# Windowed attention and a multiplicative feed-forward net in one kernel: attention of batches 2 and 3 regrouped by token halves, and more transposes by DMA

## The chip, the core and the metric

The kernel runs on one core of one Trainium2 chip. Its metric is the device time of one execution in microseconds (us). The engines of the core have these names: PE is the matrix engine (TensorE; PEld is its weight load), ACT is ScalarE, DVE is VectorE, POOL is GpSimd, SP is SyncE. POOL issues the loads, SP the DMA transposes and the stores of the output. All times are the slowest core's, and here there is one core.

## What is computed

Four batches of eight heads, 768 tokens and head size 64 go through attention in which a token sees the first four tokens (the sinks) and the 128 tokens that end with itself. The result, as 3072 rows of 512, goes through two gates, their product, and two matrices:

```python
scores = scale * np.matmul(q, k.transpose(0, 1, 3, 2))
keep = is_sink | in_window            # n_sink = 4, window = 128
scores = np.where(keep, scores, -1000000000.0)
a = softmax(scores); attn = np.matmul(a, v)
x = attn.transpose(0, 2, 1, 3).reshape(3072, 512)
h = (x @ w1) * (x @ w2) @ w3          # 512 -> 1024 -> 1024
out = h @ w_out                       # 1024 -> 512
```

## The kernel before

**Tiles.** Tokens come in blocks of 128 (six to a batch), three blocks make a chunk c of 384 tokens, and two heads make a pair r (four pairs). P is 128, NP 4, NC 2, QC 3. Scores are made with k blocks on the partitions and q along the free axis, for a pair of heads at once.

**Stages.** First w3 and w_out are folded into one matrix w3o (L333 to L389: transposes L339 and L370, matmuls L347 and L377), so that the last two products become one. For each batch then: q and k are transposed into qkT (on PE for batches 0 and 1, L427 and L450, copied out of PSUM; by DMA transposes on SP for batches 2 and 3, L468). The four sink keys of all heads stand in a small tile ksbd; its scores with q (L504) and their exponentials es (L509) belong to all heads together. A *visit* makes the scores of one or two *strips* (L547); a strip is a set of up to four blocks of 128 x 128 for two heads, and has one exponential on ACT (L560) and one masking product on DVE (L566). Attention times v (L618) gathers a chunk and a head pair in PSUM, with a column that sums the weights; DVE inverts the sum (L628) and normalizes into xs (L633). The six transposes per two head pairs that turn xs into xT are made on PE (L654, copied by L658) or, for batch 3, by three DMA transposes per chunk (L674). Each chunk then has eight pairs of gate matmuls of 384 columns (L698), a copy (L705), a product (L713), and three output blocks (L728) that are copied (L737) and stored (L745).

**Which strips.** `pieces` (L393) lists (k block, q block, number of q blocks, place in the strip) per head pair. Kind 0 (batches 0 and 1) has four strips a pair, two for each token half. Kind 1 (batches 2 and 3) has three strips a pair of 3, 4 and 4 blocks, twelve a batch, taken two at a time in six visits; the first visit needs k and q of the whole batch. The sink scores of kind 1 are one group of 512 columns ahead of the visits; those of kind 0 are two groups of 128 and 384 columns.

**Memory.** q and k of batches 2 and 3 lie in the tile `big`, over w3 and w_out, which are dead once the fold is done (L391). PSUM holds two score tiles sc, one av and three general tiles mm. Rings of tiles: three ex, six am, three xs, three xT, three o_sb.

**What sets the order.** The program is ordered when it is built. Each piece of work is an `Op` (L125) with an engine, a cost in us, dependencies and a priority; a list planner (L749 to L847) lets time pass, and on each engine emits the op that can begin first, at equal readiness the one of lower priority number (`when`, L415, spreads the attention of batch b over the projection of batch b - 1). The engines then run their instructions in this order, each in its own queue, with semaphores for the true data dependencies, which the framework puts in from the tiles that an instruction reads and writes. `Op.deps` is read by the planner. PE gaps that the planner foresees before 45 us are filled with matmuls on zeros (L807). `load` (L155) gives a load's cost, `dma["at"]` the planner's time of the DMA queue; at most eight POOL loads are in flight (L796, and lane semaphores on the chip). `unsure` (L760) adds 1.5 to 3.5 us to a load that ends after 40 us. A DMA transpose takes 1.3 us of the planner's DMA time (`TUS`, `turn`).

**The load list.** `LOADS` (L238) is the order of POOL's work by hand: `k2-4` is k of batch 2, token block 4; `v0-2` likewise; `q0-0-4` is the first half of batch 0, heads 4 to 7 (heads 0 to 3 come by SP and ACT, L210); `w3j-2-4` two column blocks of the first rows of w3, `w3-5` a row block of w3, `wo-6-8` two row blocks of w_out, `w0` to `w3` quarters of w1 and w2. `ident`, `tri` and `pick` are small constants that POOL computes. A load of q, k or v of one block moves 256 KB of float32 and writes 128 KB of bfloat16.

Of the kernel before, what the change touches and what calls it, by code (L numbers as in the profile page):

```python
# [21 lines left out]
def kernel(  # L22
# [22 lines left out]
    P = 128  # L45
# [23 lines left out]
    maskt = home("maskt", [P, 1, 7 * P])  # L69
# [55 lines left out]
    class Op:  # L125
        def __init__(self, eng, us, fn, deps=(), prio=0.0, takes=(), frees=(), lat=0.0,
                     margin=0.0, src=0.0):
            self.us_on = {eng: us} if isinstance(eng, str) else dict(zip(eng, us))
            self.eng, self.fn, self.prio = eng, fn, prio
            self.deps, self.takes, self.frees = list(deps), list(takes), list(frees)  # L130
            self.lat, self.margin, self.src = lat, margin, src
            self.done = self.slot = self.after = None
            self.serial = len(ops)
            ops.append(self)
# [18 lines left out]
    dma = dict(at=3.45, fetch=False)  # L153
# [12 lines left out]
    KA, LEAD, SPREAD = 3, -120, 0.6  # L166
    FOLD_J, FOLD_I = 990, 980
    C_MAJOR = 2
    QK_BY_DMA = (2, 3)
    X_BY_DMA = ((3, 0), (3, 1))  # L170
# [62 lines left out]
    for r in range(2):  # L233
# [4 lines left out]
    LOADS = """w3j-1-2 tri k0-0-4 q0-0-4 wo-0-1 wo-2-4 ident v0-2 w3j-2-4 w3j-6-8 w3j-0-1 wo-1-2 pick  # L238
        v0-1 wo-4-6 w3j-4-6 v0-0 w3-7 wo-6-8 w3-6 w3-5 w3-4 q0-1-0 k0-1-0 w0 w3-3 v0-5 w2 v0-3 w1
        k1-1 k1-0 w3 k1-3 q1-1 v0-4 k1-2 q1-0 q2-0 q1-2 k1-4 v1-0 q1-4 v1-5 k2-0 v1-2 v1-4 k2-3  # L240
        v1-1 q1-5 k2-2 q2-2 v1-3 q2-4 q2-1 q1-3 k2-1 k1-5 v2-5 v2-2 k2-5 v2-0 k2-4 v3-1 q2-5 q2-3
        q3-0 k3-3 v2-4 k3-2 v2-1 v2-3 k3-0 k3-4 k3-5 q3-2 k3-1 v3-2 q3-5 q3-1 v3-4 q3-3 q3-4 v3-3
        v3-0 v3-5"""

    def masks(part):
        m = maskt[:, 0, :].rearrange("p (k q) -> p k q", q=P)
        if part:
            for k in (1, 3, 4, 6):
                nc.vector.tensor_copy(m[:, k, :], tri[:])
            nc.vector.memset(m[0:4, 4:6, :], 1.0)  # L250
        else:
            for k in (0, 2, 5):
                nc.vector.tensor_scalar(m[:, k, :], tri[:], -1.0, 1.0, op0=ALU.mult, op1=ALU.add)

# [49 lines left out]
    op_mask = Op(DVE, 0.6, lambda: masks(1), [op_mask], prio=3)  # L304
    op_cols = Op(DVE, 0.35, pick_cols, [op_pick], prio=3)
# [100 lines left out]
    for b in range(B):  # L406
        kind = 0 if b < C_MAJOR else 1
# [33 lines left out]
        elif b not in QK_BY_DMA:  # L441
            for c in range(NC):
                for r in range(NP):
                    x = []

                    def tps(b=b, c=c, r=r, x=x):
                        tp = transposed(x[0].slot["mm"], 6 * P).rearrange("p (s j m) -> p s j m", s=2, m=P)
                        for s, src in ((0, kN[b]), (1, qN[b])):
                            for j in range(QC):
                                nc.tensor.transpose(tp[:, s, j, :],  # L450
                                                    src[:, QC * c + j, r * P:(r + 1) * P], ident[:])

                    def tpc(T=T, c=c, r=r, x=x):
                        copy(
                            T[:, r, :, c * TOK:(c + 1) * TOK],
                            transposed(x[0].slot["mm"], 6 * P).rearrange("p (s m) -> p s m", s=2))
                    a = Op(PE, cols(P, 6), tps,
                           [got[n, b, QC * c + j] for n in "kq" for j in range(QC)] + [op_ident] + war,
                           when((r / 4 + c) / 2 - 0.1 if kind == 0 else r / 4 + c / 50 - 0.1, 0), takes=["mm"])
                    x.append(a)  # L460
                    tp_of[c, r] = Op(EITHER, (act_us(6 * P), dve_us(6 * P, 2)), tpc, [a], base + 1, frees=[(a, "mm")])
        if b not in QK_BY_DMA:
            tdep = lambda c, r: [tp_of[c, r]] + ([tp_of[0, r]] if c else [])
        else:
            for kb in range(NB):
                for s, n, src in ((0, "k", kN), (1, "q", qN)):
# [3 lines left out]
                    tp_of[s, kb].turn = TUS  # L470
            if b + 1 in QK_BY_DMA:
                seen = []
                for o in in_big:
                    if o.batch == b:
                        seen.append(next(t for t in tp_of.values() if o in t.deps))
                    elif o.batch == b + 1:
                        o.deps += seen[:-3]
            tdep = lambda c, r: [tp_of[s, kb] for s in range(2) for kb in range(3 * c + 3)]
# [17 lines left out]
        groups = [(2, 3), (3, 6)] if kind == 0 else [(2, 6)]  # L496
        op_es = {}
        for q0, q1 in groups:
# [12 lines left out]
            cs = {(qb // QC) for qb in range(q0, q1)}  # L511
            a = Op(PE, cols(w) + 0.22, ss, [op_sk] + sum([tdep(c, r) for c in cs for r in range(NP)], []) + warv,
# [6 lines left out]
        tasks = []  # L519
        if kind == 0:  # L520
            for c in range(NC):
                for r in range(NP):
                    two = [(r, 2 * c), (r, 2 * c + 1)]
                    tasks += [two] if c or b else [[t] for t in two]
        else:
            flat = [(r, t) for r in range(NP) for t in range(3)]
            tasks = [flat[i:i + 2] for i in range(0, 12, 2)]
        block, sc_ops = {}, []
        am_left = {}
        for n_v, visit in enumerate(tasks):  # L530
            x = []
            us = 0.13
            deps = []
            for r, t in visit:
                for kb, qb, n, c in pieces[kind][t]:
                    us += cols(n * P)
                    for ch in {kb // QC, qb // QC, (qb + n - 1) // QC}:
                        deps += tdep(ch, r)
            deps = list(dict.fromkeys(deps))

            def scv(visit=visit, kind=kind, T=T, x=x):
                for i, (r, t) in enumerate(visit):
                    sc = x[0].slot["sc", i] if len(visit) > 1 else x[0].slot["sc"]
                    for kb, qb, n, c in pieces[kind][t]:
# [4 lines left out]
            s_ = Op(PE, us, scv, deps, when(n_v / len(tasks), base + 4 + 0.01 * n_v), takes=["sc"] * len(visit))  # L549
            x.append(s_)  # L550
            s_.after, last_sc[0] = last_sc[0], s_
            sc_ops.append(s_)
            for i, (r, t) in enumerate(visit):
                w = sum(n for _, _, n, _ in pieces[kind][t]) * P
# [10 lines left out]
                def msk(w=w, y=y, m0=mask_at[kind][t] * P):  # L565
                    nc.vector.tensor_mul(y[2].slot["am"][:, :, 0:w], y[1].slot["ex"][:, :, 0:w],  # L566
                                         maskt[:, :, m0:m0 + w].to_broadcast([P, 2, w]))
                m_ = Op(DVE, dve_us(2 * w, 2), msk, [e_, op_mask], base + 4 + 0.01 * n_v, takes=["am"], frees=[(e_, "ex")])
                y.append(m_)
                am_left[m_] = set()  # L570
                for kb, qb, n, c in pieces[kind][t]:
                    for j in range(n):
                        block[r, kb, qb + j] = (m_, (c + j) * P)
                        am_left[m_].add((qb + j) // QC)
# [3 lines left out]
        order = [(c, r) for c in range(NC) for r in range(NP)] if kind == 0 else \  # L578
                [(c, r) for r in range(NP) for c in range(NC)]
        xs_first, norm = {}, {}  # L580
        for n_u, (c, r) in enumerate(order):
            x = []
            deps, us, ams = [op_ones[b]], 0.0, []
            for qi in range(QC):
                qb = QC * c + qi
                for kb in (qb - 1, qb):
                    if kb >= 0:
# [4 lines left out]
                        us += 2 * 0.0295  # L592
# [4 lines left out]
            for m_ in ams:  # L597
                am_left[m_].discard(c)
# [43 lines left out]
        for c in range(NC):  # L642
            holder = [None]
            if (b, c) not in X_BY_DMA:
                evs = []
                for n_h in range(2):
# [13 lines left out]
                    a = Op(PE, cols(P, 6), xtp, [norm[c, 2 * n_h], norm[c, 2 * n_h + 1]], when(c / 2 + (n_h + 1) / 4 if kind == 0 else n_h / 2 + 0.5, base + 2.5), takes=["mm"],  # L660
# [9 lines left out]
            else:  # L670
                evs = []
                for j in range(QC):
# [6 lines left out]
                    ev.turn = TUS  # L679
# [80 lines left out]
    def unsure(at):  # L760
        return 0.0 if at < 40.0 else min(3.5, 1.5 + (at - 40.0) * 0.05)

    def wants(o):
        at = max([d.done + HOP for d in o.deps], default=0.0)
# [8 lines left out]
    def best(e):  # L773
        pick_ = None
        for o in ready[e]:
            w = wants(o) if e != POOL or o is in_order[0] else None
# [9 lines left out]
    with tc.manual_schedule():  # L786
        left, lanes = len(ops), []
        while left:
# [28 lines left out]
            turn_of[0] = e  # L817
# [4 lines left out]
            if hasattr(o, "turn"):  # L822
                dma["at"] = max(dma["at"], start + 0.6) + o.turn
                o.done = dma["at"] + 1.8
# [58 lines left out]
```

The softmax here doesn't subtract the row's maximum and nothing guards it: scores larger than these inputs give would overflow.

## Time and profile before

| What | us |
|---|---|
| median of the 13 runs shown | 201.71 (201.09 to 202.29) |
| the profiled execution | 201.41 |
| its span | 199.7 |
| PE busy | 194.2 |
| DVE, ACT, POOL busy | 111.7, 104.1, 73.1 |
| gate matmuls L698, busy | 91.2 |
| output matmuls L728, busy | 46.1 |
| scores L547, attention times v L618 (v and sinks), x transposes L654, busy | 14.9, 19.0 and 12.9, 6.0 |
| first matmul, last load issued | 1.33, 101.65 |

The profile shows one execution. The page gives each engine's busy time and its share of the span, the span in forty slices (digits are tenths; PEclk is the granted clock, and all its slices are nines), the chain of work that ended last, and groups of instructions with busy time, mean ns of one, and the idle time before them with what ended it. The mean of a matmul there includes its passage through the array and is longer than the step from one to the next, so prices of PE work are taken from the chain or from the starts in the timeline. Landing times of loads are in the views of DMA issues; those of DMA transposes are in the trace's semaphore events.

### The profile page before, as it was taken

The page shows a single profiled execution, that of the slowest core. Times are in us where ns is not written, and L with a number is a line of the kernel's source. Part 1 is how long each engine was busy: PE and PEld are TensorE (multiplying, and loading weights), DVE is VectorE, ACT ScalarE, POOL GpSimd, SP SyncE. Part 2 cuts the span into 40 slices and gives each one's busy share as a digit, 9 for nine tenths or more (in the row PEclk, how much of TensorE's full clock was granted, in tenths as well). Part 3 has the DMA queues.
Part 4 walks back from the last instruction along what each step waited for, and adds up shares of the span by engine and source line. Part 5 has one row for each costly group of instructions (what it writes and reads, how often), then busy time and mean ns, then how long its engine had stood idle before and what let it go on. Part 6 is the DMA issues. An engine that isn't in the chain of part 4 may idle for free.

```text
span 199.7 us, 4622 instructions
## 1 busy us (share of the span) xinstructions
PE 194.2 (97%) x1864; PEld 119.3 (60%) x1864; DVE 111.7 (56%) x260; ACT 104.1 (52%) x171; POOL 73.1 (37%) x96
## 2 busy tenths in 40 slices
PE   7999999999999999999999999999999999999993
PEld 7776756456665666674565765555666445665542
DVE  5591735654778877884498772448786102444200
ACT  3882467573186337652957945385761335333222
POOL 7997544977985655856820000000000000000000
PEclk9999999999999999999999999999999999999999
DMA  6999999999999999999999992002101563000133
GB/s 167 188 185 198 202 194 193 182 178 155 153 147 184 184 130 156 156 141 156 172 208 134 150 148 107 0 5 105 56 0 30 129 196 121 0 5 0 53 140 122
DMA packets 94917, 25.63 MB, mean 128 GB/s; under 512 B 83632, under 2 KB 91312, under 8 KB 94896
## 3 DMA queue, kind: packets, MB, share of 16 engines
q0 software_dynamic: 73584, 14.29, 90.9%
q1 hardware_dynamic: 20624, 10.59, 26.4%
q10 hardware_dynamic: 688, 0.46, 0.7%
q8 instruction: 14, 0.23, 0.5%
q14 instruction: 7, 0.06, 0.1%
HBM read 29.39 MB, written 6.29 MB: 179 GB/s over the span
## 4 chain that ended last, share of the span: by engine, by line
PE 91%; DMA 3%; POOL 3%; DVE 1%; issue 0%; ACT 0%; POOLq 0%
PE mm L698 42%; PE mm L728 21%; PE av L618 7%; PE sc L547 6%; PE mm L377 4%; DMA big<-in_moe_w_dram 3%; PE mm L654 2%; PE sc L347 2%; PE mm L450 2%; PE mm L370 1%; POOL big L158 1%; PE mm L347 1%; PE mm L427 1%; POOL early L158 1%; PE mm L339 1%; PE mm L504 1%
## 5 line engine op out<-in xcount | busy, mean ns | idle before, releaser
L698 PE MATMUL mm<-xT,w_sb 128*128 128x384 bf16 x512 | 91.2, 326 | 0.0
L698 PEld LDWEIGHTS <-w_sb 128*128 128x128 bf16 x512 | 47.7, 98 | 32.3 <-issue 2.2
L713 DVE TENSOR_TENSOR ab<-a_sb,mm 128x384 bf16<-128x384 f32 x64 | 35.3, 554 | 44.5 <-PE mm L698 41.9
L560 ACT ACTIVATE ex<-sc 128x768 bf16<-128x768 f32 (+2 forms) x56 | 44.8, 845 | 8.6 <-PE sc L547 7.6
L141 ACT COPY a_sb<-mm 128x384 f32<-128x384 f32 x55 | 26.4, 479 | 41.0 <-PE mm L698 25.5
L728 PE MATMUL mm<-w3o,ab 128*128 128x512 bf16 (+2 forms) x208 | 46.1, 363 | 0.0
L566 DVE TENSOR_TENSOR am<-ex,maskt 128x768 bf16<-128x768 bf16 (+2 forms) x56 | 30.7, 561 | 2.0 <-ACT ex L560 2.0
L728 PEld LDWEIGHTS <-ab 128*128 128x128 bf16 x208 | 18.8, 98 | 17.6 <-issue 0.6
L158 POOL DMA_DIRECT2D vN<-in_v_dram x24 | 21.3, 892 | 8.8 <-DMA near<-in_q_dram 2.2
L141 ACT COPY o_sb<-mm 128x512 f32<-128x512 f32 (+2 forms) x20 | 10.8, 544 | 22.1 <-PE mm L728 21.9
L618 PEld LDWEIGHTS <-am 128*128 128x128 bf16 x352 | 17.1, 97 | 3.4 <-issue 0.2
L618 PE MATMUL av<-vN,am 128*128 128x65 bf16 x352 | 19.0, 193 | 0.0
L633 DVE TENSOR_TENSOR xs<-av,rec 128x384 bf16<-128x384 f32 x32 | 17.7, 554 | 0.5
L547 PE MATMUL sc<-qkT 64*128 64x256 bf16 (+1 forms) x240 | 14.9, 243 | 0.0
L158 POOL DMA_DIRECT2D big<-in_k_dram x12 | 10.6, 887 | 6.4 <-PE sc L547 2.4
L618 PE MATMUL av<-vsb,es 128*128 128x130 bf16 x64 | 12.9, 220 | 0.0
L547 PEld LDWEIGHTS <-qkT 64*128 64x128 bf16 x240 | 8.0, 94 | 7.5 <-issue 6.1
L158 POOL DMA_DIRECT2D big<-in_q_dram x12 | 10.6, 884 | 3.2 <-DMA vN<-in_v_dram 1.9
L807 PE MATMUL mm<-zeros 128*128 128x128 bf16 x99 | 9.4, 254 | 1.3 <-DVE zeros L216 1.3
L807 PEld LDWEIGHTS <-zeros 128*128 128x128 bf16 x120 | 8.8, 113 | 2.5 <-DVE zeros L216 1.3
L141 DVE COPY qkT<-mm 128x384 bf16<-128x384 bf16 (+1 forms) x13 | 6.9, 554 | 5.5 <-PE mm L427 3.2
L377 PE MATMUL mm<-big,w3t 128*128 128x512 bf16 x40 | 9.8, 380 | 0.0
(61 smaller groups left out, 144.3 us busy)
## 6 DMA issues: line engine op xcount, KB each, us to landing
out_dram<-o_sb SPq DMA_DIRECT2D x23, 256.0 KB
vN<-in_v_dram POOLq DMA_DIRECT2D x24, 128.0 KB, 10.2
w_sb<-in_moe_w_dram POOLq DMA_DIRECT2D x8, 256.0 KB, 10.4
big<-in_q_dram POOLq DMA_DIRECT2D x12, 128.0 KB, 10.5
big<-in_k_dram POOLq DMA_DIRECT2D x12, 128.0 KB, 9.3
big<-in_moe_w_dram POOLq DMA_DIRECT2D x5, 256.0 KB, 8.6
big<-in_moe_w_out_dram POOLq DMA_DIRECT2D x3, 256.0 KB, 6.0
near<-in_k_dram POOLq DMA_DIRECT2D x6, 128.0 KB, 8.8
```

The costliest lines, as they stand in the source:

```text
L141: (nc.scalar.copy if turn_of[0] == ACT else nc.vector.tensor_copy)(out, in_)
L158: op = Op(eng, us, lambda: (nc.gpsimd if eng == POOL else nc.sync).dma_start(out=out, in_=in_), deps)
L377: nc.tensor.matmul(x[2].slot["mm"][:], x[1].slot["w3t"][:, j, :], wo_sb[:, j, :], start=(j == 0), stop=(j == KFF - 1))
L547: nc.tensor.matmul(sc[:, e, c * P:(c + n) * P], T[hp, r, 0, kb * P:(kb + 1) * P], T[hp, r, 1, qb * P:(qb + n) * P], start=True, stop=True)
L560: nc.scalar.activation(y[1].slot["ex"][:, :, 0:w], y[0].slot[key][:, :, 0:w], ACTF.Exp, scale=scale)
L566: nc.vector.tensor_mul(y[2].slot["am"][:, :, 0:w], y[1].slot["ex"][:, :, 0:w], maskt[:, :, m0:m0 + w].to_broadcast([P, 2, w]))
L618: nc.tensor.matmul(o, lhs, rhs, start=(i == 0), stop=(i == len(todo) - 1), skip_group_check=True)
L633: nc.vector.tensor_mul(xs_first[c].slot["xs"][:, :, r * P:(r + 1) * P].rearrange("p k (e d) -> p k e d", d=D), av_of(x[0].slot["av"])[:, : ...
L698: nc.tensor.matmul(pg[:, 0:TOK], w_sb[:, kk, dt * P:(dt + 1) * P], holder[0].slot["xT"][:, kk, :], start=(kk == 0), stop=(kk == NP - 1))
L713: nc.vector.tensor_mul(abh[0].slot["ab"][:, dt, :], y[1].slot["a"][:], y[2].slot["mm"][:, 0:TOK])
L728: nc.tensor.matmul(x[0].slot["mm"][:, 0:n1 - n0], abh[0].slot["ab"][:, kk, mi * P:(mi + 1) * P], w3o[:, kk, n0:n1], start=(kk == 0), stop= ...
L807: nc.tensor.matmul(view, zeros[:], zeros[:], start=True, stop=True)
```

## The change

Line numbers after a + sign belong to the changed kernel.

- **Strips of batches 2 and 3.** A kind 2 (`KINDS`) takes the place of kind 1. Its eleven strips, all of four blocks, are grouped by token half: four of the first half (k blocks 0 and 1), one diagonal strip that gathers block (2, 2) of all four head pairs, four of the second half, and two that gather k blocks 4 and 5 against q block 5 for two pairs each. They go in six visits, five of two strips and one of one. The first visit needs the first half's k and q only. Attention times v goes by chunk first, then by pair. Five more masks are copied (`late_masks`).
- **Sink scores.** In batches 1, 2 and 3 (`FUSED`) the sink scores are emitted inside a visit (visit 1 and visit 3; for batch 1 visit 1 and visit 5); batches 2 and 3 now have two groups, of 128 and 384 columns.
- **x of batch 2** is transposed by DMA like that of batch 3: six DMA transposes on SP in place of 24 PE transposes and four copies. The `ORDER` loop stands ahead of the place where batch 3's DMA transposes are entered in `tp_of`, so it finds that table empty.
- **Batch 3's q and k loads** get a dependency on the load two before (`DEEP`), beside the one on batch 2's transposes that was there.
- **The planner**: other `LEAD`, `SPREAD` and `FOLD_J`; the DMA transpose costs 0.9 of DMA time with 1.3 between two on SP (`pitch`); `unsure` is 1.0 flat; no hop between two ops of PE; the cost of an attention-value matmul is 0.031 for 0.0295.
- **The load list** is another order throughout: `ident` and `pick` first, quarters of w1 and w2 ahead of the second half of batch 0, q and k of batch 1 earlier.

```diff
-    KA, LEAD, SPREAD = 3, -120, 0.6
-    FOLD_J, FOLD_I = 990, 980
-    C_MAJOR = 2
+    KA, LEAD, SPREAD = 3, -70, 0.9
+    FOLD_J, FOLD_I = 1040, 980
+    DEEP, ORDER = 2, 1
+    FUSED = (1, 2, 3)
+    KINDS = (0, 0, 2, 2)
     QK_BY_DMA = (2, 3)
-    X_BY_DMA = ((3, 0), (3, 1))
+    X_BY_DMA = ((2, 0), (2, 1), (3, 0), (3, 1))
...
-    LOADS = """w3j-1-2 tri k0-0-4 q0-0-4 wo-0-1 wo-2-4 ident v0-2 w3j-2-4 w3j-6-8 w3j-0-1 wo-1-2 pick
-        v0-1 wo-4-6 w3j-4-6 v0-0 w3-7 wo-6-8 w3-6 w3-5 w3-4 q0-1-0 k0-1-0 w0 w3-3 v0-5 w2 v0-3 w1
-        k1-1 k1-0 w3 k1-3 q1-1 v0-4 k1-2 q1-0 q2-0 q1-2 k1-4 v1-0 q1-4 v1-5 k2-0 v1-2 v1-4 k2-3
-        v1-1 q1-5 k2-2 q2-2 v1-3 q2-4 q2-1 q1-3 k2-1 k1-5 v2-5 v2-2 k2-5 v2-0 k2-4 v3-1 q2-5 q2-3
-        q3-0 k3-3 v2-4 k3-2 v2-1 v2-3 k3-0 k3-4 k3-5 q3-2 k3-1 v3-2 q3-5 q3-1 v3-4 q3-3 q3-4 v3-3
-        v3-0 v3-5"""
+    LOADS = """ident pick w3j-0-1 q0-0-4 k0-0-4 w3j-2-4 v0-2 v0-1 w3j-1-2 tri v0-0 w3j-4-6 wo-0-1 wo-1-2
+        w3j-6-8 wo-2-4 wo-4-6 w3-4 wo-6-8 w3-7 w3-5 w3-6 w2 w0 w3 k0-1-0 q0-1-0 w3-3 w1 k1-2 k1-0
+        v0-5 v0-4 q1-0 v0-3 v1-0 q1-2 q1-4 q1-5 v1-5 v1-2 k1-1 q1-1 k2-1 k1-3 k1-4 v1-1 k1-5 q1-3
+        q2-0 k2-0 k2-2 q2-1 v2-1 v2-2 v1-4 k2-3 v1-3 q2-2 v2-0 v2-4 k2-5 q2-3 q2-5 q2-4 k2-4 q3-2
+        v2-5 q3-5 q3-0 v3-1 v3-5 q3-4 k3-1 v3-3 v3-0 v3-2 k3-4 v2-3 k3-0 q3-3 k3-3 k3-5 q3-1 k3-2
+        v3-4"""
...
+        if ORDER and b == 3 and 2 in QK_BY_DMA:
+            for c in range(NC):
+                if (2, c) in X_BY_DMA:
+                    for (s_i, kb), o in tp_of.items():
+                        if kb // QC == c:
+                            o.after = chunk_dep[2, c][1][-1]
...
-                    tp_of[s, kb].turn = TUS
+                    tp_of[s, kb].turn, tp_of[s, kb].pitch = 0.9, TUS
...
+                behind = [o for o in in_big if o.batch == b + 1]
+                for o, p in zip(behind[DEEP:], behind):
+                    o.deps.append(p)
...
+            half = [[([(r, 0, 0, 2, 0), (r, 1, 1, 2, 2)], 4) for r in range(NP)],
+                    [([(r, 2, 3, 1, 0), (r, 3, 3, 2, 1), (r, 4, 4, 1, 3)], 0) for r in range(NP)]]
+            diag = ([(r, 2, 2, 1, r) for r in range(NP)], 8)
+            rest = [([(r, kb, 5, 1, 2 * (r - r0) + kb - 4) for r in (r0, r0 + 1) for kb in (4, 5)], 0) for r0 in (0, 2)]
+            flat = half[0][:2] + [diag] + half[0][2:] + half[1][:2] + rest[:1] + half[1][2:] + rest[1:]
+            visits = [flat[i:i + 2] for i in range(0, 11, 2)]
...
     def unsure(at):
-        return 0.0 if at < 40.0 else min(3.5, 1.5 + (at - 40.0) * 0.05)
+        return 0.0 if at < 40.0 else 1.0
...
             if hasattr(o, "turn"):
                 dma["at"] = max(dma["at"], start + 0.6) + o.turn
-                o.done = dma["at"] + 1.8
+                dma["sp"] = o.done = max(start + 2.2, dma["at"] + 0.9, dma["sp"] + o.pitch)
```

## The prediction

> **What bounds the kernel now.** I read the page first: busy time of each engine, then the forty slices.
>
> ```profile
> PE 194.2 (97%) x1864; PEld 119.3 (60%) x1864; DVE 111.7 (56%) x260; ACT 104.1 (52%) x171; POOL 73.1 (37%) x96
> ...
> PE   7999999999999999999999999999999999999993
> ...
> DMA  6999999999999999999999992002101563000133
> ```
>
> TensorE (PE) is busy throughout, the clock row is nines, and the DMA engines are as full as PE until 120 us. So there are two bounds side by side, and the question is which one sets each stage. Busy PE could hide waiting, so I read PE's waits next. This is the whole list:
>
> ```profile
> PE mm L807 <- DVE zeros L216: 1.3, 1, 1.3
> PE mm L427 <- POOL ident L271: 0.3, 1, 0.3
> PE mm L339 <- DMA big<-in_moe_w_dram: 0.2, 1, 0.2
> ```
>
> PE waits for nothing after 13.2 us; before 20.4 us its gaps are filled by 120 dummy matmuls (L807). From there the span is a plain sum of PE work, and the chain of waits around the first attention of batch 2 gives its prices:
>
> ```profile
> 91.92 0.34 PE mm L654 x6
> 92.26 0.65 PE mm L698 x4
> 92.91 1.73 PE mm L728 x8
> 94.64 0.33 PE mm L504 x4
> 94.97 0.49 PE sc L547 x10
> 95.46 1.83 PE mm L728 x8
> ```
>
> A gate matmul (L698) takes 0.162 us, an output matmul (L728) 0.216, a transpose (L654) 0.056. A change between 128-row matmuls and the 64- or 32-row score matmuls costs 0.10 to 0.11: the eight L728 take 1.83 after a visit, 1.73 otherwise.
>
> Then the DMA side: the SP queue, and the last batch 2 load.
>
> ```profile
> 65.20 21.35 SPq L468 DMA_TRANSPOSE qkT<-big  x9
> 92.57 0.33 SPq L745 DMA_DIRECT2D out_dram<-o_sb  x1
> ```
>
> ```profile
> 75.86 1.89 POOL L158 DMA_DIRECT2D big<-in_q_dram  x2 [0.58 <-DMA near<-in_k_dram]
> ```
>
> ```profile
> big<-in_q_dram POOLq DMA_DIRECT2D x1, 128.0 KB, 9.4
> ```
>
> The first of those two loads is q2-3, the last batch 2 load: issued at 75.86, landed at 85.3. Its DMA transpose (the last of the nine) issues at 85.31, and by the trace's semaphore events it completes at 92.64. PE's first batch 2 instruction starts at 94.57, so the slack is 1.9 us. Batch 2 is barely off the path.
>
> **The change, part by part.** The sum is made against the profiled execution: 201.41 us, span 199.7, last matmul at about 196.24.
>
> *PE work.* Batch 2's x goes by DMA: 24 transposes fewer, four groups of 0.335, -1.34. Sink scores of batches 2 and 3 become 128 + 384 columns (0.17 + 0.28 by the L504 rows) instead of one 512 (0.33): +0.12 each, +0.24. Visits stay six per batch with the same 44 blocks of columns, and before the sinks already stood beside a visit, so fusing saves no switch: 0. ScalarE's exponentials of such a batch go from 4 x 0.815 + 8 x 1.027 = 11.5 to 11 x 1.027 = 11.3 us, VectorE's masks from 7.5 to 7.4, both lose batch 2's four x copies (0.80 or 0.56 each), and VectorE gains five small mask copies: PE, with no wait on either, hides all of it: 0. Net -1.1 us.
>
> *Start.* The dummies fall from 120 to 101 (36 to 27 of the slow first ones at 0.11), worth 1.6, but they only cover waiting. What ends that stage is a load: wo-6-8 is the 16th load in both lists, with the same 15 before it. It lands at 21.68 and PE takes it at 21.79. Moving ident and pick ahead of the first load delays POOL by some 0.8 us (rows 0.31, 0.12, 0.48); the DMA engines, idle for part of slice one only, may return some: 21.8 to 22.4, I take 21.8. The 1.6 us go to more real work done ahead of this point.
>
> *From there to batch 2's second half.* I counted the changed PE order from wo-6-8's first use to the first score matmul needing k and q of batch 2's second token half. Against the same stretch before (21.79 to 94.57, 72.8 us) it holds 20 L698 and 8 L728 fewer, 12 L654 and 22 attention-value matmuls fewer, 26 score matmuls more. By the prices above: -3.7, -1.5, -0.4, -0.4, +1.2, small ones +0.5: 4.3 us less. So PE would arrive at 21.8 + 68.5 = 90.3.
>
> *Waits in that stretch.* (a) Batch 1's second-half transposes (L450) move up: they need q1-3, now the 46th load and before the 61st. The 46th load before (v1-1) issued at 53.30 and took 8.8, landing at 62.1 with the same bytes ahead. With one DMA transpose fewer among them (below) 61.2. PE gets there at 60.6: wait 0.6 to 1.5, I take 1.0, so 91.3 at batch 2's second half. Behind this wait stands all of PE. (b) The last batch 2 load is the 63rd in both lists (q2-3 before, k2-4 after), so it lands at 85.3 again, less one DMA transpose: 31 loads of 0.87 should take 27.0 us, took 37.9 (47.42 to 85.29), and the rest, less three stores of about 0.75, over 8 to 10 transposes is about 0.9 each. k2-4 therefore lands at 84.3. Two transposes follow on SP, 1.25 apart, and the second completes 7.35 later (7.3 to 7.6 for the four issued from 79.62): 84.3 + 1.25 + 7.35 = 92.9. Ends for that latency: 2.4 for one issued with no load in flight (152.43), 4.4 behind the last loads (115.20), 8.1 at worst (106.57); I take the rows of the same stage. PE waits 1.6 us there.
>
> *The rest.* From that point the changed order holds 20 L698 (+3.2) and 8 L728 (+1.5) more, 24 L654 (-1.3) and 26 score matmuls (-1.6) fewer, sinks +0.2: +2.0 on the measured 101.67. The end of PE is 92.9 + 103.7 = 196.6, against 196.24: **+0.35 us**. The transposes leave PE, but the order moves gate work behind a point that DMA sets.
>
> *Later waits.* Batch 2's x transposes share SP with batch 3's. Its third issues behind the transpose of k3-3, whose place in the load list landed at 111.2: so at about 112.5, complete by 117 to 120; PE wants it at about 121. Batch 3's last qk transposes wait on SP behind stores of batch 1 (about 122) and finish near 128, PE wants the first at 130. Cost 0 while these slacks of 1 to 3 us hold; beyond them each late microsecond costs one.
>
> *The two-deep limit.* It and the older order between batches are entries in the planner's list, and the trace shows that such an entry binds nothing: q3-0 (the second load of the 75.86 row) was planned behind nine batch 2 transposes, and when it issued at 76.9 five of them had completed. In the changed program POOL's loads still carry only DMA-lane and PE waits. So the planner now counts on a short DMA queue which the chip won't have.
>
> The Trainium skill, "DMA: Bandwidth & Descriptors", section "Queues, rings and completion order", says that each DMA engine takes turns between queue rows, packet by packet. By that an SP transpose would take every other turn beside POOL's loads: an estimate of 3.3 us (2.4 alone and 0.9 of turns given away), and the sum would be rival 2's 200.5. The 7.3 us rows of this trace speak against it, and I go by them.
>
> **Rivals.**
> 1. *Main case*: batch 2's second half binds, between 91.5 (transposes 7.0, load early) and 93.9: -1.1 to +1.4.
> 2. *Faster*: the transposes come early, since the limit does bind or the queue is short: at 4.4 us they are there at 90.0, PE arrives unwaited at 91.3, ends at 195.0: -1.2. Without wait (a) too, -2.2. For: 4.4 was seen. Against: seen only after the last load was issued.
> 3. *Slower*: a late straggler in the loads. The q1-3 load issued at 60.20 took 13.05 us between neighbours of about 11. Such a 2.2 on k2-4 passes straight to PE, since no slack is left: +2.5. It decides from the first 0.3 us of delay. The same price stands on batch 2's x from 3 us of delay.
>
> **How the numbers follow.** Medians lie 0.3 above the profiled execution (201.71 against 201.41), so the forecast is 201.41 + 0.35 + 0.3 = **202.1 us**, the rival 2 gives 200.5 (199.5 at best), rival 3 204.2. Chances: main 0.55, faster 0.28, slower 0.17. The main case spans 200.6 to 203.1. About 0.2% (0.4 us) is what measurement can tell from no change: of the main case 0.08 falls below 201.3, 0.25 between, 0.22 above 202.1. That makes faster 0.36, same 0.25, slower 0.39. The range, 200.2 to 203.9, leaves out the ends of both rivals.
>
> **What would show it.** Right: PE waits listed on a DMA transpose of qkT near 92 us, about 1 us at an L450 group near 61, last matmul near 196.6, 101 dummies. Wrong: transposes completing in 3 to 5 us while loads are in flight, no PE wait at batch 2, or waits elsewhere (batch 2's x near 121, output copies held by stores on SP).

## The result, and the profile after

The changed kernel takes 203.19 us (median of 11 runs, 203.02 to 207.19; a twelfth took 202.60) where the kernel before takes 201.73 (48 runs, 201.09 to 202.38): a ratio of 1.0081, 95% interval 1.0065 to 1.0097. It is slower by 0.8% (0.7% by the medians). Three of the eleven runs took 205.38 to 207.19 at a mean granted clock of 0.983 to 0.992, the others at most 203.42 at 0.997 or more, and the ratio leaves out the two slowest. The forecast was 202.1, no change. The profiled execution of the changed kernel took 203.02, with a span of 201.3.

The page of the changed kernel, busy time and two rows of the forty slices:

```profile
PE 194.3 (97%) x1829; PEld 119.0 (59%) x1829; DVE 110.4 (55%) x259; ACT 103.5 (51%) x171; POOL 72.9 (36%) x96
...
PE   7989999999999999997999999999999999999993
...
DMA  6999999999999999999999997402131260120134
```

35 instructions of PE are gone and its busy time has not fallen. The PE row has dips that the one before has not: an 8 in the third slice (10 to 15 us) and a 7 in the 19th (91 to 96 us). A row of tenths says only where to look; the list of PE's waits says what ended the idle time. This is the whole list; columns are total, times, longest, in us:

```profile
PE mm L850 <- DVE zeros L219: 1.3, 1, 1.3
PE sc L585 <- DMA qkT<-big: 1.2, 1, 1.2
PE mm L523 <- DVE ksbd L502: 0.8, 1, 0.8
PE mm L437 <- DVE early L233: 0.3, 1, 0.3
```

Two lines are new: scores (L585) that wait for a DMA transpose, and sink scores (L523) that wait for VectorE's copies into ksbd. The chain of waits from 83 us on (start, us, what) leads through the first of them:

```profile
83.33 1.29 SPq L484
...
84.72 2.35 SPq L484
...
87.16 7.14 DMA qkT<-big
94.30 0.04 issue
94.34 0.34 PE sc L585 x4
```

SP issues the transpose of k2-4 at 84.72 and that of q2-4 at 87.16; the latter completes at 94.30, and PE, which had arrived at 92.99, goes on at 94.34. The load of k2-4 had landed at 84.57, but SP had been issuing one transpose after the other since 80.64 and was at the one before until 84.62: the load and SP's queue bind together here. This is the main case of the forecast in its place, 1.4 us later than forecast. Behind it the order runs without a wait to the last matmul: 198.1 by the convention of the forecast, 196.24 before.

The second new wait is in the first 15 us. PE's timeline there (start, us, instructions, idle before and what ended it), first the changed kernel:

```profile
1.33 3.06 PE L850 MATMUL mm<-zeros 128*128 128x128 bf16 x27 [1.33 <-DVE zeros L219]
4.43 0.98 PE L437 MATMUL mm<-ident,early 128*64 128x128 bf16 x12
...
7.85 1.78 PE L850 MATMUL mm<-zeros 128*128 128x128 bf16 x15
...
10.37 0.86 PE L437 MATMUL mm<-ident,early 128*64 128x128 bf16 x24
...
14.25 0.24 PE L523 MATMUL mm<-qkT,ksbd 128*32 128x128 bf16 x4 [0.82 <-DVE ksbd L502]
```

and the kernel before:

```profile
5.68 0.93 PE L427 MATMUL mm<-ident,early 128*64 128x128 bf16 x24 [0.33 <-POOL ident L271]
...
9.35 1.40 PE L807 MATMUL mm<-zeros 128*128 128x128 bf16 x22
...
11.23 0.24 PE L504 MATMUL mm<-qkT,ksbd 128*32 128x128 bf16 x4
```

Fifteen matmuls on zeros take 1.78 us at 7.85 in the changed kernel, twenty-two take 1.40 at 9.35 in the one before. From start to start the step is 0.107 us there and 0.056 here: the changed PE runs at half rate until 10.2 us, the one before only through its first group of zeros, to 5.2. (The clock row of the page shows nines for both: the trace's record of the granted clock begins only when it rises to 1.00, at 10.25 and 5.72 us, so in this first stage the steps tell.) The sink scores, at 11.23 before, come at 14.25. VectorE's timeline says why:

```profile
6.66 1.02 DVE L142 COPY qkT<-mm 128x384 bf16<-128x384 bf16 x2 [0.98 <-PE mm L437]
10.77 1.30 DVE L509 TENSOR_TENSOR vsb<-vst,pick 128x512 bf16<-128x512 f32 x2 [3.09 <-DMA vst<-in_v_dram]
11.98 0.56 DVE L256 TENSOR_SCALAR maskt<-tri 128x128 bf16<-128x128 bf16 x3
12.29 1.02 DVE L142 COPY qkT<-mm 128x384 bf16<-128x384 bf16 x2
...
13.92 0.28 DVE L502 COPY ksbd<-qkT 64x16 bf16<-64x16 bf16 x2
```

The products vsb = vst x pick wait 3.1 us for the small loads of v's sink rows, and ten other VectorE operations stand between them and the ksbd copies. With `pick` ready early, the planner put these products early; by its own formula it counts on the small loads at about 8 us (an estimate), and by the trace their last packet ends at 9.8 (10.38 before, where the products stood behind ksbd at 11.16).

### The profile page after: what moved, and what is told of

Its sections match the earlier page's. It is cut to its first block, busy times and chain, and to the rows that moved or that the text cites. A ratio compares the mean times of both kernels' runs of the same rounds, so it can differ in the third digit from the quotient of the medians.

```text
span 201.3 us, 4579 instructions
## 1 busy us (share of the span) xinstructions
PE 194.3 (97%) x1829; PEld 119.0 (59%) x1829; DVE 110.4 (55%) x259; ACT 103.5 (51%) x171; POOL 72.9 (36%) x96
## 4 chain that ended last, share of the span: by engine, by line
PE 84%; DMA 7%; DVE 3%; SPq 2%; issue 2%; ACTq 0%; ACT 0%; DVEq 0%
PE mm L741 38%; PE mm L771 20%; PE av L661 7%; PE sc L585 5%; PE mm L387 4%; DMA qkT<-big 4%; DMA a_sb<-in_q_dram 2%; SPq L484 2%; PE sc L357 2%; PE mm L380 1%; PE mm L697 1%; PE mm L460 1%; DMA vst<-in_v_dram 1%; PE mm L357 1%; PE mm L437 1%
## 5 line engine op out<-in xcount | busy, mean ns | idle before, releaser
L741 PE MATMUL mm<-xT,w_sb 128*128 128x384 bf16 x512 | 89.7, 326 | 0.0
L741 PEld LDWEIGHTS <-w_sb 128*128 128x128 bf16 x512 | 48.1, 98 | 32.5 <-issue 1.5
L771 PE MATMUL mm<-w3o,ab 128*128 128x512 bf16 (+2 forms) x208 | 45.1, 363 | 0.0
L142 ACT COPY a_sb<-mm 128x384 f32<-128x384 f32 x52 | 24.9, 479 | 34.3 <-DVE ab L756 23.6
L142 ACT COPY o_sb<-mm 128x512 f32<-128x512 f32 (+2 forms) x25 | 13.8, 552 | 30.8 <-PE mm L771 30.7
L585 PE MATMUL sc<-qkT 64*128 64x128 bf16 (+1 forms) x240 | 15.6, 248 | 1.2 <-DMA qkT<-big 1.2
L585 PEld LDWEIGHTS <-qkT 64*128 64x128 bf16 x240 | 8.2, 95 | 6.9 <-issue 5.4
L671 DVE RECIPROCAL rec<-av 128x6 f32<-128x6 f32 x32 | 6.2, 193 | 10.2 <-PE av L661 10.2
L850 PE MATMUL mm<-zeros 128*128 128x128 bf16 x90 | 8.7, 267 | 1.3 <-DVE zeros L219 1.3
L387 PE MATMUL mm<-big,w3t 128*128 128x512 bf16 x40 | 9.3, 380 | 0.0
L850 PEld LDWEIGHTS <-zeros 128*128 128x128 bf16 x101 | 7.9, 119 | 2.3 <-DVE zeros L219 1.3
## 6 DMA issues: line engine op xcount, KB each, us to landing
vN<-in_v_dram POOLq DMA_DIRECT2D x24, 128.0 KB, 10.2
```

The costliest lines, as they stand in the source:

```text
L142: (nc.scalar.copy if turn_of[0] == ACT else nc.vector.tensor_copy)(out, in_)
L387: nc.tensor.matmul(x[2].slot["mm"][:], x[1].slot["w3t"][:, j, :], wo_sb[:, j, :], start=(j == 0), stop=(j == KFF - 1))
L585: nc.tensor.matmul(sc[:, e, c * P:(c + n) * P], T[hp, r, 0, kb * P:(kb + 1) * P], T[hp, r, 1, qb * P:(qb + n) * P], start=True, stop=True)
L741: nc.tensor.matmul(pg[:, 0:TOK], w_sb[:, kk, dt * P:(dt + 1) * P], holder[0].slot["xT"][:, kk, :], start=(kk == 0), stop=(kk == NP - 1))
L771: nc.tensor.matmul(x[0].slot["mm"][:, 0:n1 - n0], abh[0].slot["ab"][:, kk, mi * P:(mi + 1) * P], w3o[:, kk, n0:n1], start=(kk == 0), stop= ...
L850: nc.tensor.matmul(view, zeros[:], zeros[:], start=True, stop=True)
```

## The experiments

All twelve were run beside the kernel before; ratios are against its runs in the same place. Theory D is that the DMA transposes of batch 2's second half set the end, so that the late start is hidden behind them; theory S that the start sets it. The edits with `hold_for` reorder one queue without a new plan: the planner's order is kept, and the instructions of an operation are written into its engine's queue only right after those of another one (`_emit` does this, `hold_for` holds the pairs; the edits are shown shortened). In the traces of these and of e1_warm to e3_both the order of every queue is that of the changed kernel except for the moves named and the matmuls on zeros added.

**The start, the load order, and both** (e1_warm, e2_loads, e3_both).

```diff
-                    for i in range(n):
+                    for i in range(n + (13 if free[PE] < 1.5 else 0)):
                         nc.tensor.matmul(view, zeros[:], zeros[:], start=True, stop=True)
```
```diff
-        q2-0 k2-0 k2-2 q2-1 v2-1 v2-2 v1-4 k2-3 v1-3 q2-2 v2-0 v2-4 k2-5 q2-3 q2-5 q2-4 k2-4 q3-2
+        q2-0 k2-0 k2-2 q2-1 v2-1 v2-2 v1-4 k2-3 v1-3 q2-2 k2-5 q2-3 q2-5 q2-4 k2-4 v2-0 v2-4 q3-2
```

> The changed kernel with 13 more matmuls on zeros in the very first group (27 to 40), everything else in the same order. In the changed kernel the first 27 steps and the real work up to 10.2 us ran at 0.107 us a 128-column step, and PE reached the first score matmul of batch 2's second half at 93.0 where 90.3 to 91.3 was forecast; it then waited 1.3 us until a DMA transpose completed at 94.23. Theory D (the DMA transposes of batch 2's second half set the end, the slow start is hidden behind them): steps of 0.056 from about 5.4 us, PE at batch 2's second half at 90.3 to 91.5, a wait of 2.5 to 3.9 us there in place of 1.3, time 202.6 to 203.3 (203.2 before). If the instruction fetch at 84.3 moves away from the last two transposes, they complete 1.1 earlier: 202.0. Theory S (the slow start sets the end): the 2.6 us come back whole, 200.4 to 200.8. Theory N (the extra matmuls change no step): 203.2 and PE still slow to 10 us.

> The changed kernel with two loads of v (v2-0, v2-4) moved behind k2-4, the last of batch 2's q and k loads; PE, DVE, ACT and SP keep their order. Theory D: k2-4 lands 1.7 us earlier (about 82.8), the last transpose completes at 92.4 or so, PE arrives unwaited at 93.0, and the time falls by the 1.3 us of the wait: 201.8 to 202.0. Theory S (the start sets the end, the wait is not what is left): 203.2. If the two v loads now come late for the attention at 95.3, some of it returns: 202.5.

> Both of the edits before: 13 more matmuls on zeros at the start, and the two loads of v behind k2-4. Theory D: PE could arrive at batch 2's second half at 90.4 to 91.5, the transposes are there at 92.4, so 200.9 to 201.5; neither edit alone gives this. Theory S: as with the extra matmuls alone, 200.4 to 200.8 in both.

Measured: 204.84 (1.0124, 1.0081 to 1.0166), 203.42 (1.0081, 1.0050 to 1.0113) and 203.08 (1.0060, 1.0036 to 1.0084). With 13 more matmuls PE stepped at 0.056 from 5.7 us (7.1 in e3_both), as wanted, and gained nothing: its first use of wo-6-8, 24.44 in the changed kernel, came at 24.39 in e3_both and at 26.27 in e1_warm. Theory S in the form "slow steps" fell. One reason is the wait for ksbd, which VectorE's queue sets whatever PE does; the other is that the 13 matmuls themselves take 1.4 us. In e1_warm the wait was 2.1 us, and it cost twice. The line in its list of waits:

```profile
PE mm L523 <- DVE ksbd L502: 2.1, 1, 2.1
```

and the stretches around it (columns: stretch and length in us, busy time of PE, PEld, DVE, ACT, POOL with instructions, granted clock, DMA share, GB/s):

```profile
12.00:14.70 2.70, 0.61 (x11) 0.43 (x8) 2.65 (x13) 0.29 (x1) 1.41 (x3) 1.00 1.50 192
14.70:16.00 1.30, 1.27 (x22) 1.11 (x22) 1.30 (x4) 0.92 (x3) 1.30 (x3) 0.99 1.36 201
16.00:18.00 2.00, 2.00 (x26) 1.61 (x24) 1.19 (x9) 1.51 (x3) 1.40 (x3) 0.50 1.25 205
18.00:20.40 2.40, 2.35 (x33) 1.87 (x29) 1.89 (x6) 1.67 (x3) 1.49 (x2) 0.71 1.19 208
```

Two microseconds of waiting are followed by a granted clock of 0.50 from 16.0 to 19.4 us, though PE is busy then. With 1.5 us of the same wait (e3_both) the clock stayed at 1.00. The six runs of e1_warm differ in this: two at a mean clock of 1.000 took 202.75 and 203.79, the four others, at 0.975 to 0.992, 204.79 to 209.73. So e1_warm's 204.84 is not a clean price of the 13 matmuls; e3_both, at 0.992 to 1.000, is nearer to one. In e2_loads (its profiled execution, 204.62, is the longest of its eight) k2-4 landed at 83.1 in place of 84.6, and the last transpose completed no earlier, at 94.95: its issue, at 86.22, was the sixth in a row on SP, which took 2.1 and 2.9 us for the last two. So moving two loads was not enough to test theory D: SP's queue stood in their place.

**Fewer matmuls on zeros in the kernel before** (e4_before_cold): the same line, `range(n - (9 if free[PE] < 1.5 else 0))`.

> The kernel before with 9 matmuls on zeros fewer in its first group (36 to 27, as many as in the changed kernel), everything else in the same order. If a full 4 us of matmuls ahead of the first real work is what brings PE to its full rate: steps of 0.107 until 8 to 10 us in place of 5.7, and since PE waits for nothing after 13.2 us in the kernel before, all of the delay reaches the end: 203.2 to 204.4 against 201.7. If these matmuls only cover waiting, as the prediction took it: 201.7 and steps of 0.056 from the first real work.

Measured: 202.62 (1.0044, 1.0023 to 1.0065). PE's timeline:

```profile
1.33 3.06 PE L807 MATMUL mm<-zeros 128*128 128x128 bf16 x27 [1.33 <-DVE zeros L216]
5.71 1.49 PE L427 MATMUL mm<-ident,early 128*64 128x128 bf16 x24 [1.31 <-POOL ident L271]
...
7.42 1.17 PE L807 MATMUL sc<-zeros 128*128 128x128 bf16 x9
```

The 24 transposes that took 0.93 us in the kernel before take 1.49, and nine matmuls on zeros that took 0.67 take 1.17: nine matmuls fewer in the first group leave PE at half rate to about 9 us (9.4 by the record of the clock). The matmuls on zeros are no mere filling. Of the 1.5 to 2.7 us expected, 0.9 reached the end.

**VectorE's queue, four loads, and both** (e5_start, e6_loads4, e7_start_loads).

```diff
+    hold_for = {svs[0][0]: svs[0][1], svs[1][0]: svs[0][1]}       # e5, e7: vsb of batches 0, 1 after ksbd of batch 0
+    hold_for = {got["v", 2, i]: got["k", 2, 4] for i in (1, 2, 0, 4)}   # e6, e7: these loads after k2-4
...
-            o.fn()
+            _emit(o, hold_for, held, turn_of)
```

> The changed kernel with one move in DVE's queue: the two products vsb = vst x pick (L509), which waited for the small loads of v's sink rows until 10.8 us and held 11 DVE operations behind them, stand behind the two ksbd copies (L502) instead. No other queue changes. Theory B (this wait in DVE's queue is what starves PE at the start): the ksbd wait of PE at 13.4 to 14.2 goes, PE is 1.0 us earlier from there to batch 2's second half (91.9 instead of 92.9) and then waits for the DMA transposes 1.0 longer, so that the end does not move: 203.0 to 203.4 (theory D), or 202.2 if the transposes come sooner too. Rival (PE's slow clock alone makes the start late): PE at 14.25 for the sink scores as before, and no change anywhere.

> The changed kernel with four loads of v of batch 2 (v2-1, v2-2, v2-0, v2-4) moved behind k2-4 in POOL's queue, all other queues in the same order. k2-4 is now the 63rd load in place of the 67th and lands at about 81. Theory D (the transposes of batch 2's second half set the end): they are complete at 89.5 to 91.5, PE arrives at 93.0 unwaited, and the wait of 1.3 us is gone: 201.7 to 202.0. If DMA transposes complete no faster than one in 1.4 us beside loads, whatever the place of the last load (in the run with two loads moved the last one completed at 94.9 although its load had landed 1.5 us earlier): the wait stays at 0.5 to 1.5 and the time at 202.5 to 203.2.

> Both of the edits before in one kernel: the vsb products behind ksbd in DVE's queue, four loads of v behind k2-4. Theory D with B: PE arrives at batch 2's second half at 91.9 and the transposes are there: 200.7 to 201.1, 2.3 below the changed kernel and below the kernel before. If only the start counts: 202.2 as in the best case of the first; if only the transposes: 201.8.

Measured: 203.90 (1.0091, 1.0058 to 1.0124), 203.02 (1.0057, 1.0034 to 1.0080) and 202.07 (1.0021, 0.9999 to 1.0042). The traces of the first and third differ in the four loads alone and share the start. PE's timeline at batch 2's second half, e5_start:

```profile
93.08 0.45 PE L585 MATMUL sc<-qkT 64*128 64x256 bf16 x6
95.09 0.34 PE L585 MATMUL sc<-qkT 64*128 64x256 bf16 x4 [1.56 <-DMA qkT<-big]
```

and e7_start_loads:

```profile
93.10 0.61 PE L585 MATMUL sc<-qkT 64*128 64x256 bf16 x10
93.64 0.82 PE L741 MATMUL mm<-xT,w_sb 128*128 128x384 bf16 x4
```

PE arrives at the same time, and the wait of 1.6 us is there in the one and gone in the other. Theory D holds for this wait. The four loads alone (e6_loads4) missed the 201.7 to 202.0 of theory D all the same and fell in the range of its rival, and what took the rest is not shown: its one trace is of an execution of 205.44 us, longer than all its others, with a clock of 0.50 from 14.7 to 18.1 us and no wait for these transposes. But the DVE edit did not bring PE forward as expected (it comes to the waiting matmul at 93.4, in the changed kernel at 92.99): the wait for ksbd fell from 0.8 to 0.2, and PE waited 1.1 for an exponential on ACT instead, whose buffer the mask product behind vsb freed late. And e7_start_loads has a wait that the changed kernel has not, the third line here, from the head of its list of waits:

```profile
PE mm L850 <- DVE zeros L219: 1.3, 1, 1.3
PE sc L585 <- ACT ex L603: 1.1, 1, 1.1
PE mm L741 <- DMA xT<-xs: 1.1, 1, 1.1
```

The gates of batch 2 (L741) wait at 122 us for x, which this change makes by DMA.

**The same with the 13 matmuls, then with one more edit on SP** (e8_all3, e11_sp): four transposes of batch 3 go behind the third x transpose of batch 2's first chunk.

```diff
-    hold_for = {svs[0][0]: svs[0][1], ...}
+    tp3 = lambda n, kb: next(o for o in ops if SP in o.us_on and got[n, 3, kb] in o.deps)
+    hold_for = {svs[0][0]: svs[0][1], ...,
+                **{tp3(*n): chunk_dep[2, 0][1][-1] for n in (("k", 4), ("k", 0), ("q", 3), ("k", 3))}}
```

> The same with 13 more matmuls on zeros in the first group, so that PE is at 0.056 a step from about 7.6 us (as the run with these matmuls alone showed) in place of 10.2. With the wait in DVE's queue gone, the faster steps should now show: PE another 0.5 to 1.5 us earlier at batch 2's second half (90.5 to 91.4). Theory D: 200.0 to 200.8 if the transposes are there by then, the same as the run without the matmuls if they are not. If PE's slow steps at the start cost nothing in any case: as the run without them.

> The kernel with vsb behind ksbd on DVE, 13 more matmuls on zeros and four loads of v moved, and one more edit on SP alone: the three DMA transposes of x of batch 2's first chunk go one after the other, and the four transposes of batch 3's k and q that stood between them (k3-4, k3-0, q3-3, k3-3) follow. All other queues in the same order. In the run without this edit the third x transpose was issued at 114.61, complete at 121.84, and PE waited 1.0 for it (0.8 to 1.1 in three runs). Theory (transposes on SP are next in line to set the end): they are issued at about 104.5, 105.7 and 107, complete by 116, the wait goes, and the time falls from 202.0 to 201.0 (200.7 to 201.3). If batch 3's transposes are then late for PE at 130: some 0.5 returns. Rival (the wait at 120 is filled by something else, output copies or stores): 202.0.

Measured: 201.98 (1.0000, 0.9977 to 1.0024) and 201.34 (0.9960, 0.9942 to 0.9977). The 13 matmuls alone (e8_all3 against e7_start_loads) gained nothing that the intervals tell. SP's timeline in e8_all3:

```profile
104.45 1.22 SPq L717 DMA_TRANSPOSE xT<-xs  x1
105.77 4.31 SPq L484 DMA_TRANSPOSE qkT<-big  x2
110.13 1.28 SPq L717 DMA_TRANSPOSE xT<-xs  x1
111.50 3.06 SPq L484 DMA_TRANSPOSE qkT<-big  x2
114.61 1.44 SPq L717 DMA_TRANSPOSE xT<-xs  x1
```

and in e11_sp:

```profile
103.67 4.81 SPq L717 DMA_TRANSPOSE xT<-xs  x3
108.58 5.97 SPq L484 DMA_TRANSPOSE qkT<-big  x4
```

The third x transpose completes at 114.39 in place of 121.89, and PE's wait for it, 0.8 us in e8_all3, is off the list: it was the place in SP's queue. The ratio fell by 0.4%, which is 0.8 us.

**VectorE once more** (e12_am): vsb of batch 0 behind the first mask product, that of batch 1 behind the first four.

> The same as the one with the edit on SP, and on DVE the first vsb product one place further back, behind the first mask product (am0), the second behind the first four mask products. In the runs with vsb just behind ksbd, ACT's exponential waited for am0 until 14.5 us and PE for that exponential 0.6 to 1.1 us at 15.2. If the start still sets PE's arrival everywhere behind it, PE gains 0.6 to 0.8 from 15 us on, and the time with it: 200.2 to 200.6. If the transposes of batch 2's second half (complete at 91 to 93 in these runs) are there too late for it: 200.8 to 201.1. If the start is filled otherwise: no change from the run with the edit on SP.

Measured: 201.04 (0.9953, 0.9933 to 0.9974), 202.08 for the kernel before beside it. The wait for the exponential is gone, and yet PE takes wo-6-8, the mark of the forecast, at 23.84, no earlier than in e11_sp (23.39): the expectation fell, and no gain beyond the interval is left. The mark is 2.1 us behind the kernel before, but 1.5 of this is no loss: the changed order has 22 attention-value matmuls (0.83 us) and 12 transposes (0.67) more ahead of it. The 110 matmuls on zeros ahead of it take 9.7 us where the 120 before took 10.1. Nothing between this mark and the end waits for more than 0.16 us in these two traces, so what the start loses reaches the end. Both e11_sp and e12_am are faster than both kernels, and they keep all that the change does to the strips, the sinks and x.

**Parts undone** (e9_x2_pe, e10_kinds): x of batch 2 on PE, and three strips a pair; here the planner orders the rest anew.

```diff
-    X_BY_DMA = ((2, 0), (2, 1), (3, 0), (3, 1))
+    X_BY_DMA = ((3, 0), (3, 1))            # e9
...
-    KINDS = (0, 0, 2, 2)
+    KINDS = (0, 0, 1, 1)                   # e10
```

> One part of the change undone: x of batch 2 is transposed on PE again (24 matmuls and four copies), DMA transposes for batch 3's x only; the planner orders the rest anew. Theory D: the waiting at the start and for the transposes of batch 2's second half lies before this point and stays, PE carries 1.34 us of transposes and four changes more: 204.4 to 204.8. Rival X (the six DMA transposes of batch 2's x cost as much as they save, by the wait for x at 119 to 122 us that three of the runs showed with 0.8 to 1.1 us, and by their share of the DMA engines): 203.0 to 203.6, as the changed kernel.

> Another part undone: batches 2 and 3 in three strips a pair (kind 1 as before), twelve strips in six visits of which the first needs q and k of the whole batch; x of both by DMA, load list and planner constants as changed. The planner orders the rest anew. The strips themselves are worth 0.24 us of PE work by the forecast. Theory D: the first visit now needs all of batch 2's transposes (94.2 in the changed kernel), and the planner, which counts on them earlier, has less gate work left to put before it: a wait of 3 us or more, 204 to 206. If the strips by halves matter little because the planner fills the place: 202.8 to 203.4.

Measured: 205.22 (1.0153, 1.0111 to 1.0194) and 209.27 (1.0338, 1.0292 to 1.0383). Without either part the changed order is slower. How much of the first is x itself is not shown: four of its six runs have a mean clock of 0.990 to 0.992, its profile shows 2.0 us of waiting for ksbd and a clock of 0.50 at 16 to 18 us, and the two runs at 0.999 and 1.000 took 203.82 and 205.17. They speak against rival X and are too few for a price. In the second the place was not the expected one. Its profiled execution is the longest of its six (210.88; the only one at a clock of 0.999 took 207.46), and in it PE waits nothing at batch 2's scores, 1.6 us in four waits for exponentials at 129 to 133 us, and 2.6 us for batch 2's x. The head of its list of waits:

```profile
PE mm L741 <- DMA xT<-xs: 2.6, 1, 2.6
```

and the stretches behind that wait, in the columns named above:

```profile
134.00:136.00 2.00, 0.00 (x0) 0.00 (x0) 0.00 (x0) 0.28 (x1) 0.00 (x0) 0.69 0.45 90
136.00:138.00 2.00, 1.83 (x6) 0.87 (x7) 0.90 (x2) 0.00 (x0) 0.00 (x0) 0.50 0.33 66
138.00:140.00 2.00, 2.00 (x8) 0.90 (x7) 1.88 (x4) 0.00 (x0) 0.00 (x0) 0.50 0.04 8
```

Again the clock is 0.50 after the wait: a gate matmul takes 0.32 us from 136 to 141, so 16 of them cost 2.5 us on top of the 2.6. How much of the 3.4% the strips themselves are, apart from the new order and the clock, stays open.

## Why the prediction was right and wrong, step by step

**PE's work: right.** From the first use of wo-6-8 (24.44) to batch 2's second half (92.99) PE takes 68.55 us; the forecast counted 68.5. From there to the end it takes 103.8; the forecast said 103.7. The counts of instructions are right to the last one. That the sums came out to 0.1 us over 170 is in part luck: 20 gate matmuls at 0.162 are 3.2 us, where the forecast has 3.7 in one sum and 3.2 in the other, eight output matmuls 1.7 and not 1.5, 12 transposes and 22 attention-value matmuls 0.7 each and not 0.4. By its own prices the first stretch would be 68.1 and the second 103.9.

**Start: the step that failed.** "What ends that stage is a load [...] I take 21.8." The load landed at 22.13, within the forecast's bounds, and PE came to it at 24.44. PE's list of waits before has no wait there, so nothing had shown that the load sets the place (nor are all 15 loads ahead of it the same: w3-4 stands for w3-7). The step "they only cover waiting", said of the matmuls on zeros, was wrong: with 27 of them, PE kept 0.107 a step until 10.2 us in this execution (in three of the eight traces with 27 only to 4.5 to 5.1, see the last section). And the move of `pick` to the head of the list was priced as 0.8 us of POOL; what it moved was vsb in VectorE's queue, in front of all the masks and copies that PE's first work needs. The diff of the load list does not show this; the order of VectorE's queue does, and the forecast did not follow it through the first 15 us. By the starts in the two timelines, up to this point PE does 1.5 us more of work that the kernel before does later, takes 1.6 longer for the same transposes and scores at half rate, waits 0.8 for ksbd, and spends 1.2 less on matmuls on zeros: together the 2.65 us. Only the first and the last of these four were in the forecast.

**Wait (a): size wrong because of the start.** q1-3 landed at 61.17 (forecast 61.2), but PE reached L460 at 63.30. Cost 0 in place of 1.0.

**Wait (b): right place, a term too small.** k2-4 landed at 84.57 (forecast 84.3). The forecast added 1.25 for the second issue and 7.35 for its passage. The passage took 7.14; the issue of k2-4's transpose took 2.35 us, and began 0.15 late, and the next began 0.09 behind it. Together 94.30 in place of 92.9, and this is nearly the whole of the miss: 94.34 + 103.8 = 198.1, where 92.9 + 103.7 = 196.6 was forecast. The tail behind the last matmul was 0.25 shorter than before, so 203.02 was measured where these terms give 201.41 + 1.86 - 0.25.

**The late start cost little by itself.** Had PE come at 90.3, it would have waited for 94.30 all the same. The edits of the start alone brought nothing (e1_warm, e5_start), the four loads alone little (1.0057), both together 1.0021 (e7_start_loads) and 1.0000 (e8_all3) against the 1.0081 of the changed kernel. With two loads moved (e3_both against e2_loads) the intervals overlap.

**Later waits at 0: right for this kernel, thin.** No wait stands behind 94.34. Of the sixteen updates that batch 2's third x transpose makes of its semaphore, fifteen came by 119.9 (forecast 117 to 120) and the last at 121.44, and PE wanted it at 122.6: 1.2 us of slack. In e7_start_loads PE came at 121.6, that transpose completed at 122.8, and PE waited: "beyond them each late microsecond costs one" was the right price, and the place in SP's queue the cause (e11_sp).

**The two-deep limit binds nothing: right.** When q3-0 issued at 80.88, q3-2 and q3-5 (landed 85.36 and 89.20) were still in flight, so three of batch 3 at once.

**The transposes' latency: right.** 7.1 to 8.2 us for the last four of batch 2, and 7.0 to 9.4 in the experiments' traces at the same place; rival 2, with 4.4, is out. The forecast read some completions early: by the last update the last transpose before is there at 92.86 and not 92.64, and the slowest, issued at 102.84, took 9.3 us, not 8.1 at worst. The estimate of 3.3 us that the forecast worked out from the Trainium skill ("DMA: Bandwidth & Descriptors", "Queues, rings and completion order") is out by the same rows; whether the turns between queue rows or the size of a turn is at fault, no run here shows.

## What to carry to other kernels

When a list of loads or a planner is changed, read every engine's new order for the stage that has no slack, above all for an operation that waits on a transfer and stands in front of others in an in-order queue: here one product that nobody needed until 16 us held VectorE for 3 us. Where two paths end within a microsecond of each other, as PE and the transposes did at 93 and 94, repairing one shows little until the other is repaired too, and then the third in line appears. And a mark in the order, such as the first use of a load, compares two kernels only when the same work lies ahead of it. Order a queue of DMA issues by when the results are wanted: four transposes that could wait cost about 0.4% in front of three that could not.

## What the runs showed of the hardware

PE begins at half rate (0.107 us a 128-column step). By the traces' record of the granted clock it came to 1.00 at 5.7 us in the kernel before, with 36 unbroken matmuls ahead (3.9 us), and at 4.8 to 7.1 in the five traces with 40. With 27 (2.9 us) it came at 9.4 to 10.8 in five traces, but at 4.5 to 5.1 in three (e6_loads4, e9_x2_pe, e10_kinds): the same start differs from one execution to the next. Every stretch of one clock that the record shows whole is a multiple of 3.41 us long (3.41 in e1_warm, 6.83 in e10_kinds, 191.15 in the changed kernel). The Trainium skill ("TensorE: Matmul & The Clock Gate", "Part 1: The HAM clock gate") tells of a free-running window of about 3.4 us that must be busy, which agrees. It names an idle window of that length for the way back; here waits of 2.0, 2.0 and 2.1 us in a row (e9_x2_pe, e10_kinds, e1_warm) were enough for a clock of 0.50 over 3.41 us, one of 2.6 for 6.83, and three of 1.5 to 1.6 were not. So an early full rate does not help while something else holds PE: where it came early and the vsb products had their old place, the wait for ksbd grew from 0.8 to 1.9 to 2.1 us and the clock fell (e1_warm, e6_loads4, e9_x2_pe, e10_kinds).

SP issues a DMA transpose in 1.25 us, but in up to 4.0. Over the fourteen traces 69 issues took more than 1.8 us, and 58 of them overlap a packet of instruction fetch (8 or 16 KB; one began at 84.3 in the changed kernel); of the 417 shorter ones 80 do. No run moved the fetch alone, so this is an association and not shown as the cause.
